# Gated mix of an S5 scan and hedgehog linear attention: the last two output tiles scaled in halves by two engines

## The chip, the cores and the metric

The kernel runs on one core of a Trainium2 chip. TensorE (PE) multiplies into PSUM, VectorE (DVE) and ScalarE (ACT) move and transform tiles between PSUM and SBUF, GpSimd (POOL) does small set-up work, and SyncE (SP) issues transfers; ACT can issue transfers from its own queue too. The metric is device time in microseconds, the median of several executions. Before the change it is 155.21 us (three executions, 154.76 to 155.4).

## What is computed

The input `x` has 2048 rows of 512 features. Two branches read it, and a gate mixes them row by row. Cut to what matters:

```python
g = sigmoid((x * gate_w).sum(-1, keepdims=True))
# branch a: a diagonal complex recurrence over the 2048 rows
h[t] = Lam_bar * h[t-1] + B_bar @ x[t]
a = 2.0 * real(hseq @ Cmat.T) + x * Dskip
# branch b: linear attention, 32 heads of 16, softmax feature maps of +p and -p
num = phi_q @ (phi_k.T @ v);  den = phi_q @ phi_k.sum(rows) + 1e-6
b = (num / den) @ wo
out = g * a + (1 - g) * b
```

All inputs and the output are bfloat16. The kernel takes `g` out of the sum: it accumulates `a` and `b * (1 - g) / g` in one PSUM tile and multiplies the whole by `g` at the end.

## The kernel before the change

The 2048 rows are cut into 16 tiles of 128 rows, numbered n = 0 to 15 in the order in which the output is made. Each stage is a Python generator that records a few instructions and yields; the string `ORDER` (line 24) is a list of tokens written out by hand, and line 804 walks it: each token runs its generator one step on. So the place of a token in the list sets where its instructions stand in each engine's queue. Behind a token, `@4` names the PSUM bank, `:D` gives a copy or scaling to VectorE instead of ScalarE, and `:A` sends a store from ScalarE's queue instead of SP's.

Early tokens load and transpose weights and `x`, build the recurrence, and run the key side of the attention. The last third makes the output, tile by tile, with three stages:

- `y` (`st_y`, line 711) opens the PSUM tile `py` (128x512, float32, one bank) and adds branch a to it: products at line 717 and the skip term at 722.
- `o` (`st_o`, line 725) makes the attention output of the tile: products into `pn` (736), logarithm `ld` of the denominators and copy `nu` of the numerators out of the same bank (739, 740), their quotient `on` (744), and its transpose `oT`. For n up to 11 a transfer does the transposing (758); for tiles 12 to 15 TensorE does it into `po` (753), and one copy, `oT` from `po` (755, through `evac`, lines 119 and 121), brings it to SBUF.
- `t` (`st_t`, line 761) has three steps: the products of `oT` with `Wo`, added to `py` (765); scaling of `py` by the gate column of `G` into the SBUF tile `ot` (769 on ScalarE, 771 on VectorE); and one store of `ot`, 128 KB, to the output in HBM (773).

The products of tile n can start only when its `oT` copy is done. The list ends with the products of tile 13, then the transposes of tile 14, the three steps of tile 15, the copy of tile 14 on VectorE, the products of tile 14, scaling and store of tile 13, and scaling and store of tile 14. In this ending all three scalings are on ScalarE; the stores of tiles 15 and 13 are issued by SP, that of tile 14 by ScalarE. Behind everything stands the closing of the program (line 843 in the profile): SP waits for the semaphore of every transfer lane, then all engines meet at a barrier.

Each transfer issued by ACT or SP takes the next of eight semaphore lanes in turn, so the lane of a store follows from its place among all transfers.

Of the kernel before, what the change touches and what calls it, by code (L numbers as in the profile page):

```python
# [10 lines left out]
ALU = mybir.AluOpType  # L11
# [3 lines left out]
BF16 = mybir.dt.bfloat16  # L15
# [5 lines left out]
P = 128  # L21
# [27 lines left out]
o10 S3 y14@3 S3 y14 t7 t7:D t8 y14 t8 y15@0 o11@4 S3 o11 o11@1 t9 o12@4 o11:D o11 S3 o10 o10 o12 o12@1 o12 o12 t9:D  # L49
o11 y15 o13@4 o13:D o13@6 t6:A o13 o13 o11 o12 y10@1 o14@4 y15 o14:D o12@6 t9 o12:D t7:A t1 y10 y10 o13 o15@4 o15  # L50
o15@6 t4:A t5 o15 o15 t8 o15 t12 t12 t12:A t10 o14@4 o14 o14 t10:D o13@6 t11 o15@2 o15 t10 o13:D t11 t11:A y13 t13 o14
o14@1 t15 t15 t15 o14:D t14 t13 t13 t14 t14:A
"""
H_VECTOR = tuple((r, j) for r in (1, 2, 4, 5, 6) for j in range(4))
OT_PE = (12, 13, 14, 15)
# [13 lines left out]
def kernel(  # L69
# [18 lines left out]
    nc = tc.nc  # L88
    _, S, D = A_x.shape
# [5 lines left out]
    NTI = S // P  # L95
# [10 lines left out]
    out_par = out2.rearrange("(a c r) d -> c r a d", r=NR, c=P)  # L106
    VT = nc.vector.tensor_tensor
    VS = nc.vector.tensor_scalar
# [70 lines left out]
    G = const.tile([P, NTI], F32, name="G")  # L179
# [280 lines left out]
    pools = {}  # L460
# [300 lines left out]
    def st_t(n):  # L761
        ti = order[n]
        py, oT = live["py", n], live["oT", n]
        for g in range(HG):
            MM(out=py[:], lhsT=oT[:, g, :], rhs=Wo[:, g, :], start=False, stop=(g == HG - 1))  # L765
        yield
        ot = pools["op"][1].tile([P, D], BF16, name="ot", bufs=14)
        if sel["eng"] == "act":
            nc.scalar.mul(out=ot[:], in_=py[:], mul=G[:, ti:ti + 1])  # L769
        else:  # L770
            VS(out=ot[:], in0=py[:], scalar1=G[:, ti:ti + 1], scalar2=None, op0=ALU.mult)
        yield
        sel["q"].dma_start(out=out_par[:, ti // 2, ti % 2, :], in_=ot[:])
        yield
# [17 lines left out]
    for n in range(NTI):  # L792
        st.update({f"k{n}": st_k(n), f"v{n}": st_v(n), f"q{n}": st_q(n), f"y{n}": st_y(n), f"o{n}": st_o(n), f"t{n}": st_t(n)})
# [54 lines left out]
```

## Time and profile before

| what | value |
|---|---|
| median of the executions | 155.21 us |
| the profiled execution's own time | 155.28 us |
| its span, first to last instruction | 153.2 us |
| granted TensorE clock, mean | 0.995 |
| TensorE matmul busy | 146.2 us, 95% |
| VectorE busy | 132.4 us, 86% |
| ScalarE busy | 129.2 us, 84% |
| HBM read and written | 2.64 MB and 2.10 MB |

The span is what the trace covers; the profiled execution's own time is 2.1 us more, which lies outside the trace. A row of the timeline is: start in us from the span's beginning, duration in us, engine, line, operation, output tile <- inputs, and in brackets the idle time of the engine before it with what ended that idle time. A `q` behind an engine's name (ACTq, SPq) marks its instruction queue: issuing a transfer, or waiting. A group row has the number of instructions, then total busy us and the mean ns of one, then the idle time before them.

### The profile page before, as it was taken

Reading aid. Unit: us, or ns where it says so; the run is one execution under the profiler, and the core shown is the slowest. Engines: PE = TensorE matmul, PEld = TensorE weight load, DVE = VectorE, ACT = ScalarE, POOL = GpSimd, SP = SyncE. Lnnn points to the kernel's source line nnn. Section 1 sums busy time; section 2 is a strip of 40 time slices with the busy share of each in tenths; the row PEclk is TensorE's granted clock in tenths of the full one; section 3 lists DMA queues with packets and bytes.
Section 4 is the critical chain, followed back from the end, with each engine's and each line's share of the span. In section 5 each row is a group of like instructions: output and inputs, shape, how many; then the busy total and the mean of one; then the engine's idle time right before and its main releaser. Section 6 shows DMA issues by size and latency. Waiting matters only on the chain.

```text
span 153.2 us, 3361 instructions
## 1 busy us (share of the span) xinstructions
PE 146.2 (95%) x1236; PEld 95.0 (62%) x1254; DVE 132.4 (86%) x303; ACT 129.2 (84%) x279; POOL 15.8 (10%) x43
## 2 busy tenths in 40 slices
PE   7899999999999999999999999999999999999990
PEld 7644434788878985869867656555554455555540
DVE  3799999999999999999999999999999958717520
ACT  3489998999998999999998999699498998627562
POOL 8239980000000000000000000000000000000000
PEclk9999999999999999999999999999999999999997
DMA  4875995534445699930000007711278859969842
GB/s 116 164 218 97 223 178 112 103 75 103 103 107 78 129 230 178 166 115 4 0 0 4 0 0 169 74 37 34 42 98 147 176 122 189 162 129 206 247 143 103
DMA packets 50848, 17.55 MB, mean 115 GB/s; under 512 B 44176, under 2 KB 50832, under 8 KB 50832
## 3 DMA queue, kind: packets, MB, share of 16 engines
q1 hardware_dynamic: 48976, 15.75, 53.8%
q10 hardware_dynamic: 1696, 1.57, 3.2%
q8 instruction: 10, 0.16, 0.5%
q0 software_dynamic: 160, 0.01, 0.2%
q14 instruction: 6, 0.05, 0.1%
HBM read 2.64 MB, written 2.10 MB: 31 GB/s over the span
## 4 chain that ended last, share of the span: by engine, by line
PE 78%; SPq 10%; DMA 7%; issue 1%; ACT 1%
PE pgq L601 18%; PE py L717 16%; PE pq L475 9%; PE py L765 8%; SPq L229 8%; PE pv L475 4%; PE ph L668 4%; PE pk L475 4%; DMA xT<-in_A_x_dram 4%; PE kvacc L578 3%; DMA phT<-EEq 3%; PE pn L736 3%; PE pgq L606 2%; PE py L722 2%; PE pgq L608 2%; SPq L284 1%
## 5 line engine op out<-in xcount | busy, mean ns | idle before, releaser
L601 PE MATMUL pgq<-xT,BT 128*128 128x256 bf16 x256 | 31.5, 272 | 0.0
L475 PEld LDWEIGHTS <-xT 128*128 128x128 bf16 x192 | 18.2, 98 | 18.3 <-DMA xT<-in_A_x_dram 0.7
L601 PEld LDWEIGHTS <-BT 128*128 128x128 bf16 x256 | 24.6, 98 | 4.1
L138 ACT ACTIVATE EEk<-EEk 128x1024 bf16<-128x1024 bf16 x20 | 20.4, 1080 | 0.0
L119 ACT CAST uv<-pgq 128x512 bf16<-128x512 f32 x28 | 15.9, 605 | 0.5 <-PE pgq L601 0.4
L475 PE MATMUL pv<-Wv,xT 128*128 128x512 bf16 x59 | 15.5, 379 | 0.3
L475 PE MATMUL pq<-Wq,xT 128*128 128x512 bf16 x60 | 15.4, 379 | 0.2
L765 PE MATMUL py<-Wo,oT 128*128 128x512 bf16 x62 | 15.3, 379 | 0.1
L475 PE MATMUL pk<-Wk,xT 128*128 128x512 bf16 x62 | 14.7, 379 | 0.3 <-DMA xT<-in_A_x_dram 0.2
L138 ACT ACTIVATE EEq<-EEq 128x1024 bf16<-128x1024 bf16 x12 | 11.7, 1042 | 0.3 <-DVE EEq L527 0.3
L769 ACT ACTIVATE ot<-py,G 128x512 bf16<-128x512 f32 x12 | 7.9, 686 | 4.5 <-PE py L765 4.3
L138 ACT ACTIVATE ld<-pn 128x16 f32<-128x16 f32 x32 | 6.1, 191 | 5.7 <-PE pn L736 4.6
L590 ACT ACTIVATE phT<-X,dgB 128x512 bf16<-128x512 bf16 x16 | 10.7, 725 | 0.0
L119 ACT CAST nu<-pn 128x256 bf16<-128x256 f32 x27 | 9.9, 380 | 0.0
L119 ACT CAST vx<-pv 128x512 bf16<-128x512 f32 x16 | 9.1, 604 | 0.4 <-PE pv L475 0.4
L548 DVE TENSOR_TENSOR EEk<-EEk,rck 128x4096 bf16<-128x4096 bf16 (+1 forms) x5 | 9.3, 1858 | 0.0
L744 DVE TENSOR_TENSOR on<-nu,rd 128x512 bf16<-128x512 bf16 x16 | 6.7, 421 | 2.8 <-ACT rd L138 1.6
L765 PEld LDWEIGHTS <-oT 128*128 128x128 bf16 x64 | 5.7, 97 | 5.3 <-DMA oT<-on 0.5
L119 ACT CAST Xq<-pq 128x512 bf16<-128x512 f32 x16 | 8.9, 608 | 0.0
L119 ACT CAST Xq<-pk 128x512 bf16<-128x512 f32 x15 | 8.6, 598 | 0.4 <-PE pk L475 0.4
L736 PEld LDWEIGHTS <-phT 128*128 128x128 bf16 x128 | 6.2, 97 | 3.8 <-DMA phT<-EEq 1.4
L511 DVE TENSOR_TENSOR smk<-smk 128x512 bf16<-128x512 bf16 (+4 forms) x18 | 8.1, 448 | 0.1
(178 smaller groups left out, 321.2 us busy)
## 6 DMA issues: line engine op xcount, KB each, us to landing
X<-HM SPq DMA_DIRECT2D x8, 256.0 KB, 4.5
out_dram<-ot ACTq DMA_DIRECT2D x8, 128.0 KB, 2.5
out_dram<-ot SPq DMA_DIRECT2D x8, 128.0 KB, 2.2
C2r<-in_B_wqkv_dram ACTq DMA_DIRECT2D x2, 256.0 KB, 3.8
Wv<-in_B_wqkv_dram SPq DMA_DIRECT2D x1, 512.0 KB, 4.0
Bn<-in_A_B_re_dram SPq DMA_DIRECT2D x1, 512.0 KB, 5.7
Bn<-in_A_B_im_dram SPq DMA_DIRECT2D x1, 512.0 KB, 6.8
Wo<-in_B_wo_dram SPq DMA_DIRECT2D x1, 512.0 KB, 4.3
```

Of the source, the lines that this page charges most:

```text
L119: nc.scalar.copy(out=out_ap, in_=in_ap)
L138: ins = nc.scalar.activation(**kw)
L229: nc.sync.dma_start_transpose(out=xT[:, :, ti * P:(ti + 1) * P], in_=x_res[ti // 2, ti % 2])
L475: MM(out=pt[:], lhsT=xT[:, kt, ti * P:(ti + 1) * P], rhs=W[:, kt, :], start=(kt == 0), stop=(kt == KT - 1))
L511: VT(out=dst, in0=cur[:, :, :, 0:n, :], in1=cur[:, :, :, n:2 * n, :], op=op)
L548: VT(out=E5, in0=E5, in1=rc.to_broadcast([P, L, 2 * NB, Dh, 4]), op=ALU.mult)
L590: nc.scalar.mul(out=t_, in_=x_, mul=c_)
L601: MM(out=pg[:, h, :], lhsT=BT[:, kt, 2 * j + h, :], rhs=xT[:, kt, r * NC:(r + 1) * NC], start=(h == 0 and kt == 0), stop=(r % 2 == 0 and k ...
L717: MM(out=py[:], lhsT=hs(r, t, slice(a * P, (a + 1) * P)), rhs=C2B[t], start=(t == 0), stop=False)
L736: MM(out=pn[:, 4 * m:4 * m + 4, :].rearrange("p h e -> p (h e)"), lhsT=ph[:, 4 * hf + m, :], rhs=KVm[:, 4 * hf + m, :], start=(m == 0), st ...
L765: MM(out=py[:], lhsT=oT[:, g, :], rhs=Wo[:, g, :], start=False, stop=(g == HG - 1))
L769: nc.scalar.mul(out=ot[:], in_=py[:], mul=G[:, ti:ti + 1])
```

## The change

The copy of tile 14's `oT` on VectorE (`o14:D`) moves in the list from behind the three steps of tile 15 to in front of them. For tiles 14 and 15 the scaling is cut into two halves of 256 columns: ScalarE scales columns 0 to 255 into a tile `oh0`, VectorE scales columns 256 to 511 into a tile `oh1`, each tile with two buffers; and each half has a store of its own (64 KB), the first from ScalarE's queue, the second from SP's. Tile 13 keeps its one scaling on ScalarE and its one store on SP.

```diff
-o14@1 t15 t15 t15 o14:D t14 t13 t13 t14 t14:A
+o14@1 o14:D t15 t15 t15 t14 t13 t13 t14 t14
 """
...
             MM(out=py[:], lhsT=oT[:, g, :], rhs=Wo[:, g, :], start=False, stop=(g == HG - 1))
         yield
+        if n >= NTI - 2:
+            ha = [pools["op"][1].tile([P, D // 2], BF16, name=f"oh{c}", bufs=2) for c in range(2)]
+            nc.scalar.mul(out=ha[0][:], in_=py[:, 0:D // 2], mul=G[:, ti:ti + 1])
+            VS(out=ha[1][:], in0=py[:, D // 2:D], scalar1=G[:, ti:ti + 1], scalar2=None, op0=ALU.mult)
+            yield
+            for c, q in enumerate((nc.scalar, nc.sync)):
+                q.dma_start(out=out_par[:, ti // 2, ti % 2, c * (D // 2):(c + 1) * (D // 2)], in_=ha[c][:])
+            yield
+            return
         ot = pools["op"][1].tile([P, D], BF16, name="ot", bufs=14)
```

The order of the built programs differs only in this ending. TensorE's list is the same, instruction for instruction. ScalarE's ends with: half of 15, its store, scaling of 13, half of 14, its store. VectorE's ends with: copy of 14, half of 15, half of 14. SP's ends with: half store of 15, store of 13, half store of 14, then the closing waits.

## Prediction

> **What bounds the kernel now.** I read the page first, for what carries the whole.
>
> ```profile
> span 153.2 us, 3361 instructions
> PE 146.2 (95%) x1236; PEld 95.0 (62%) x1254; DVE 132.4 (86%) x303; ACT 129.2 (84%) x279; POOL 15.8 (10%) x43
> PE 78%; SPq 10%; DMA 7%; issue 1%; ACT 1%
> ```
>
> TensorE carries 78% of the chain that ended last, and the change leaves its list alone. So only the ending can move. The chain of waits, from 148 us on:
>
> ```profile
> 147.88 0.45 PE py L765 x2
> 148.32 0.02 issue
> 148.34 0.89 ACT ot L769 x2
> 149.23 0.27 issue
> 149.50 0.69 ACT ot L769
> ```
>
> The products of tile 15 release the first scaling, and from there the chain stays on ScalarE. The timeline of the same stretch shows who waits (windows cut short, so that equal rows are not merged):
>
> ```profile
> 147.06 0.39 PE L753 MATMUL po<-ident,on 128*128 128x128 bf16 x4
> 147.48 0.42 DVE L121 COPY oT<-po 128x512 bf16<-128x512 bf16 x1 [1.06 <-PE po L753]
> 148.14 1.03 PE L765 MATMUL py<-Wo,oT 128*128 128x512 bf16 x4
> 148.34 0.69 ACT L769 ACTIVATE ot<-py,G 128x512 bf16<-128x512 f32 x1 [1.00 <-PE py L765]
> 148.93 1.25 ACT L769 ACTIVATE ot<-py,G 128x512 bf16<-128x512 f32 x2
> 149.06 0.33 SPq L773 DMA_DIRECT2D out_dram<-ot  x1
> 149.63 0.33 SPq L773 DMA_DIRECT2D out_dram<-ot  x1
> 149.50 0.69 ACT L769 ACTIVATE ot<-py,G 128x512 bf16<-128x512 f32 x1
> 150.22 0.34 ACTq L773 DMA_DIRECT2D out_dram<-ot  x1
> ```
>
> The scalings of 15, 13 and 14 start at 148.34, 148.93 and 149.50. TensorE's last product ends at 149.17, so tile 14 waits 0.33 us for ScalarE, which is still at tiles 15 and 13. ScalarE bounds this end: three scalings in a row, then one store, its landing, and the closing.
>
> **The change, part by part.** First the move of tile 14's copy. TensorE's transposes end at 147.45 and the copy starts at 147.48, with VectorE idle for 1.06 us before. Nothing else is in VectorE's queue in front of it, before or after: cost nothing. Its cover is its place ahead of the new half of tile 15: behind that half it would start after 149.2 instead of 147.48, and tile 14's products with it.
>
> Next, the halves. Durations of like operations, from the groups by shape:
>
> ```profile
> L769 ACT ACTIVATE ot<-py,G 128x512 bf16<-128x512 f32 x12 | 7.9, 686 | 4.5 <-PE py L765 4.3
> L119 ACT CAST vx<-pv 128x512 bf16<-128x512 f32 x16 | 9.1, 604 | 0.4 <-PE pv L475 0.4
> L119 ACT CAST nu<-pn 128x256 bf16<-128x256 f32 x27 | 9.9, 380 | 0.0
> L771 DVE TENSOR_SCALAR ot<-py,G 128x512 bf16<-128x512 f32 x4 | 3.0, 750 | 4.2 <-PE py L765 4.1
> L121 DVE CAST Wk<-pf 128x512 bf16<-128x512 f32 x2 | 1.4, 686 | 0.0
> L121 DVE CAST nu<-pn 128x256 bf16<-128x256 f32 x5 | 2.0, 423 | 2.6 <-ACT ld L138 2.6
> ```
>
> No row has a 256-column scaling. ScalarE's lies between its 256-column copy, 0.38, and that plus what scaling costs over copying at 512 columns (686 - 604 = 82 ns), 0.46. I take 0.45, near the end that is the same operation. VectorE's lies between 0.42 and 0.42 + (750 - 686) = 0.49; I take 0.46. Halving the columns saves far less than half the time.
>
> Then, do the halves run side by side? The last row above speaks against it. VectorE's copy `nu` reads other columns of `pn` than ScalarE's `ld`, needs nothing that `ld` makes, and yet 2.6 us of its idle time ended on `ld`. In the built list of the changed kernel (which has no times) VectorE's two halves likewise name ScalarE's semaphore, not TensorE's: reads of one PSUM tile by two engines are put behind one another. The Trainium skill, PSUM — Partial Sum Buffer, section "PSUM bank collisions raise a hardware error", says why: two engines on one bank and quadrant of partitions collide even when both only read, and at other addresses, so the compiler orders them; it would make the halves serial, as the `nu` row does, and separate destination tiles would not lift that. Without the rule, side by side, the sum would be the second rival's.
>
> So VectorE's half comes behind ScalarE's, after a hand-over:
>
> ```profile
> 145.55 0.41 ACT L138 ACTIVATE rd<-ld,nge 128x128 bf16<-128x128 f32 x1
> 146.00 0.43 DVE L744 TENSOR_TENSOR on<-nu,rd 128x512 bf16<-128x512 bf16 x1 [0.18 <-ACT rd L138]
> ```
>
> From ScalarE's end at 145.96 to VectorE's start at 146.00: 0.04 us. Scaling a tile then takes 0.45 + 0.04 + 0.46 = 0.95 us where it took 0.69.
>
> Next, the store that ScalarE now issues between tiles 15 and 13. It must wait for its half to finish, and whatever stands behind it in ScalarE's queue waits too: tile 13's scaling, then tile 14's half, then VectorE's half, the last store and the closing. What it costs is seen where the kernel already does it:
>
> ```profile
> 144.12 0.69 ACT L769 ACTIVATE ot<-py,G 128x512 bf16<-128x512 f32 x1
> 144.53 0.29 PE L736 MATMUL pn<-KVm,phT 128*128 128x68 bf16 x4
> 144.84 0.34 ACTq L773 DMA_DIRECT2D out_dram<-ot  x1
> 145.22 0.18 ACT L138 ACTIVATE ld<-pn 128x16 f32<-128x16 f32 x1 [0.41 <-PE po L753]
> ```
>
> The `ld` had its `pn` at 144.82 and the scaling ended at 144.81, yet `ld` began at 145.22, 0.04 after the issue ended. One store between two ScalarE instructions is a gap of 0.41 us.
>
> Now the sum on the path. Half of 15 from 148.34 to 148.79; gap 0.41; tile 13 starts at 149.20 (before: 148.93). Half of 14 follows 0.57 later, the distance of 13 and 14 before (149.50 - 148.93): 149.77 to 150.22. By then the products (149.17) are long done, so TensorE stays out of it. VectorE's half: 150.26 to 150.72. SP issues the last store about 0.03 later, the distance from 150.19 (end of tile 14's scaling) to 150.22: 150.75. SP's queue is free then: half store of 15 at about 149.3, tile 13's store at 149.20 + 0.68 + 0.03 = 149.9, each 0.33. So the last store is issued 0.53 us later than now. ScalarE's half store of 14 goes at 150.25 and is ahead of it.
>
> Next the landing (issues in windows around the last two SP stores, then around ScalarE's; the GB/s row is the stretch 149.9 to 151.7 in slices of 45 ns):
>
> ```profile
> out_dram<-ot SPq DMA_DIRECT2D x2, 128.0 KB, 1.9
> out_dram<-ot ACTq DMA_DIRECT2D x1, 128.0 KB, 2.0
> GB/s 205 319 364 364 319 364 341 273 228 69 23 0 68 182 319 341 364 364 341 364 296 183 69 23 0 23 205 296 341 341 364 364 364 296 205 91 23 0 0 0
> ```
>
> The last store's bytes move in the last 12 filled slices, 0.5 us of its 2.0; the rest is latency. No row has a 64 KB store of 512-byte rows. If bytes set its time it saves half of 0.5, landing in 1.75; if the 128 rows set it, nothing, 2.0. I take 1.86, between them. Landing is 152.61 instead of 150.22 + 2.0 = 152.22: 0.39 later.
>
> Last the closing. SP's waits in three windows, 150 to 150.25, then two rows from 152.2 to 152.4:
>
> ```profile
> L843 SPq EVENT_SEMAPHORE  x4: 17/28/28, 150.0 to 150.2; - x4
> L843 SPq EVENT_SEMAPHORE  x2: 28/28/28, 152.2 to 152.3; - x2
> L843 SPq DRAIN  x1: 13/13/13, 152.4 to 152.4; - x1
> ```
>
> SP goes through the lanes in a fixed order. Four that had long landed took three steps in 0.2 us, 0.067 each. Now the last store's lane is the seventh of eight: after it lands SP passes one more, then drains. The two new stores turn the lanes on: in the built list the last half store gets the first lane, named in the very first closing wait. After it lands six more passes follow where one did: five more, 5 x 0.067 = 0.33 us. By the rounding a step is 0.03 to 0.1, so 0.15 to 0.5.
>
> Sum: 0.39 + 0.33 = 0.72 us later. The profiled execution's own 155.28 becomes 156.0; it stands 0.07 above the median, so against that 155.93: I say 155.9. With all low ends (0.38 twice, 0.42, 1.75, 0.15) the sum is 0.26, with all high ends (0.46 twice, 0.49, 2.0, 0.5) 1.08: 155.5 to 156.3 by the median.
>
> **The rivals.** (1) The halved stores land later. Over all 16 stores of the kernel:
>
> ```profile
> DMA to landing us min/median/max: 1.9/2.3/3.9
> ```
>
> Tile 13's store and both of 14's now run within 0.85 us on two queues. If the last lands in the median 2.3, that adds 0.44: 156.4, slower. It decides when the bytes of one still move as the next begins. For it: the median itself. Against it: the last stores, already only 0.6 apart, land in 1.9 and 2.0.
>
> (2) The halves run side by side after all. VectorE's half of 14 would be done by 149.7, the last stores go out at 150.25, 0.50 earlier than forecast: 155.4, not measurably slower. For it: separate output tiles. Against: the `nu` row and the built list. It needs VectorE's half to start before ScalarE's ends.
>
> (3) The closing passes cost nothing, because the barrier waits for something else: 0.39 alone, 155.6. Against it: in the trace the drain comes 0.1 to 0.2 behind the last landing's wait.
>
> **How the numbers follow.** About 0.5%, 0.78 us, is what a measurement of this kernel can tell from no change, so the border lies at 155.99, just above my forecast. Chances: forecast 0.57, later landing 0.20, closing free 0.15, side by side 0.05, something that gains outright 0.03. Slower by over 0.5%: all of the first rival and some 0.25 of the forecast's 0.57, 0.45. Faster by over 0.5%: 0.03, since no term has an end below zero but for the second rival's. Within: 0.52. The range 155.4 to 156.4 takes in every bound and the second and third rivals.
>
> **What would show it.** Right: VectorE's half of 14 begins just after ScalarE's half ends; ScalarE stands 0.4 us between half 15 and tile 13; the last store goes out from SP near 150.75; about six closing waits follow its landing. The copy of tile 14 must stay at 147.5. Wrong: both halves starting together, a last issue before 150.3, or any row before 148 us that moves by more than some 0.1 us.

## The result, and the profile after

The changed kernel took 156.05 us (median of 11 executions, 155.63 to 157.47) against 155.21 for the kernel before: ratio 1.006, 95% interval 1.0034 to 1.0087. The forecast was 155.9. The profiled execution took 156.05 us over a span of 154.0.

A second set of executions of the same changed kernel, again beside the kernel before, gave 1.0029 (1.0004 to 1.0053). So the loss was measured twice, as 0.6% and as 0.3%; the two intervals overlap from 0.34% to 0.53%.

The timeline of the changed kernel's ending (start us, duration us, engine, line, operation, count, idle time before). Its lines 769 and 770 are the two halves, 773 their stores, 778 and 782 scaling and store of tile 13, and 852 the closing:

```profile
147.77 0.42 DVE L121 COPY oT<-po 128x512 bf16<-128x512 bf16 x1 [1.00 <-PE po L753]
148.63 0.47 ACT L769 ACTIVATE oh<-py,G 128x256 bf16<-128x256 f32 x1 [1.00 <-PE py L765]
149.13 0.34 ACTq L773 DMA_DIRECT2D out_dram<-oh  x1
149.14 0.48 DVE L770 TENSOR_SCALAR oh<-py,G 128x256 bf16<-128x256 f32 x1 [0.95 <-ACT oh L769]
149.52 0.69 ACT L778 ACTIVATE ot<-py,G 128x512 bf16<-128x512 f32 x1 [0.42 <-ACT oh L769]
149.65 0.33 SPq L773 DMA_DIRECT2D out_dram<-oh  x1
150.10 0.47 ACT L769 ACTIVATE oh<-py,G 128x256 bf16<-128x256 f32 x1
150.23 0.33 SPq L782 DMA_DIRECT2D out_dram<-ot  x1
150.60 0.34 ACTq L773 DMA_DIRECT2D out_dram<-oh  x1
150.60 0.48 DVE L770 TENSOR_SCALAR oh<-py,G 128x256 bf16<-128x256 f32 x1 [0.98 <-ACT oh L769]
151.12 0.33 SPq L773 DMA_DIRECT2D out_dram<-oh  x1
```

Each VectorE half (149.14, 150.60) begins when ScalarE's half of the same tile ends, although its products were done earlier. Between ScalarE's half of 15 and tile 13 stands the store's gap, 0.42 us. The last store leaves SP at 151.12.

All starts are later here (148.63 where it was 148.34); that arises ahead of the ending, in work that the change does not touch. Over these two kernels and all runs below whose code ahead of the ending is the same, that first start lies anywhere between 148.34 and 149.86 in the one profiled execution each. So I compare endings: from the start of tile 15's first scaling to the end of the span. An ending falls into three terms: to the issue of the last store, from there to its landing, and the closing from there to the end.

| kernel | to issue | landing | closing | ending us |
|---|---|---|---|---|
| before | 1.87 | 2.02 | 0.98 | 4.87 |
| changed | 2.49 | 1.65 | 1.28 | 5.41 |

(Each from the trace's times of that scaling, of the last store's issue and last semaphore write, and of the last instruction, to 0.01 us; rounding can leave 0.01.) The ending is 0.54 us longer, 0.35% of the time.

The last half store's landing (the row of the issues from 151.0 to 151.2), the rate of all transfers in slices of 45 ns from 150.6 to 152.4, and SP's closing waits from 151.4 on:

```profile
out_dram<-oh SPq DMA_DIRECT2D x1, 64.0 KB, 1.6
```

```profile
GB/s 341 251 194 91 23 0 0 0 0 0 137 250 319 387 319 364 341 341 228 228 262 319 307 251 205 103 12 0 0 11 148 228 330 284 228 160 57 12 0 0
```

```profile
L852 SPq EVENT_SEMAPHORE  x7: 28/28/1289, 151.5 to 153.1; - x7
L852 SPq DRAIN  x1: 13/13/13, 153.2 to 153.2; - x1
```

The last nine filled slices are the last half store's bytes: they move in 0.4 us, behind a short pause. The first closing wait holds SP for 1289 ns, from 151.5 until the last store has landed; six more passes (a pass is SP's wait for one lane; these lanes have landed by then) follow, the last starting at 153.1, before SP drains at 153.2. Before the change the last landing left one pass. And the groups by shape give what the trace of before had no row for:

```profile
L769 ACT ACTIVATE oh<-py,G 128x256 bf16<-128x256 f32 x2 | 0.9, 470 | 1.0 <-PE py L765 1.0
L770 DVE TENSOR_SCALAR oh<-py,G 128x256 bf16<-128x256 f32 x2 | 1.0, 484 | 1.9 <-ACT oh L769 1.9
```

Half the columns cost ScalarE 0.47 where the whole cost 0.69, and VectorE 0.48 where it cost 0.75.

### The profile page after: what moved, and what is told of

Its sections match the earlier page's. It is cut to its first block, busy times and chain, and to the rows that moved or that the text cites. A ratio compares the mean times of both kernels' runs of the same rounds, so it can differ in the third digit from the quotient of the medians.

```text
span 154.0 us, 3366 instructions
## 1 busy us (share of the span) xinstructions
PE 146.8 (95%) x1236; PEld 96.0 (62%) x1254; DVE 133.4 (87%) x305; ACT 129.0 (84%) x279; POOL 15.8 (10%) x43
## 4 chain that ended last, share of the span: by engine, by line
PE 73%; DVE 14%; DMA 6%; ACT 3%; issue 1%; ACTq 1%; DVEq 0%
PE pgq L601 18%; PE py L717 13%; PE pq L475 9%; PE py L765 7%; PE pv L475 4%; PE ph L668 4%; DMA oT<-on 3%; PE kvacc L578 3%; DMA phT<-EEq 3%; PE pgq L606 2%; DVE mnk L511 2%; PE spin L821 2%; PE pn L736 2%; DVE mxk L511 2%; PE py L722 2%; PE pgq L608 2%
## 5 line engine op out<-in xcount | busy, mean ns | idle before, releaser
L778 ACT ACTIVATE ot<-py,G 128x512 bf16<-128x512 f32 x10 | 6.8, 686 | 4.1 <-PE py L765 3.6
```

## The experiments

All endings in this section are split as in the table above. The runs with a ratio were compared with executions of the kernel before on the same chip; there its median was up to 0.75 us above the first set's, so ratios can be compared and times cannot.

**The changed kernel again**

> The changed kernel unaltered, on the same chip as the next three. If the loss is the ending alone (0.54 us of the span), the ratio to before is about 1.0035 and the ending is again 5.4. If something ahead of the ending is slower too, as the first profile hints (tile 15's first scaling at 148.63 in place of 148.34), the ratio stays at 1.006 or above.

Ratio 1.0029 (1.0004 to 1.0053), ending 2.49 + 1.65 + 1.27 = 5.41. The ending repeats to 0.01 us, and the ratio this time holds what the ending alone would give (0.35%); it is no second sign that something ahead of the ending is slower. In this trace the first scaling starts late again, at 148.59. But the kernel before has a single trace, and the spans of its executions in this set range from 153.0 to 155.5 us, so that start tells nothing.

**The copy back behind tile 15**

```diff
-o14@1 o14:D t15 t15 t15 t14 t13 t13 t14 t14
+o14@1 t15 t15 t15 o14:D t14 t13 t13 t14 t14
```

> The change without the move: the copy of tile 14 stands again behind tile 15's half on VectorE. The ending (from the start of tile 15's first scaling to the end of the span) is 4.87 us in the kernel before and 5.41 in the changed one. My theory, that the move is worth nothing by itself but shields the copy from the new half: VectorE's half of 15 ends about 0.99 after ScalarE's half begins, the copy then takes 0.42, tile 14's four products 0.86, its halves and the store as before: ending about 6.3, time about 156.9. Rival, the place in the list does not matter because the copy's inputs are ready early: 5.4, time 156.0.

Ratio 1.0117 (1.0068 to 1.0166), ending 3.47 + 1.65 + 1.27 = 6.40, near the 6.3 of the theory. The timeline shows why:

```profile
149.76 0.48 DVE L770 TENSOR_SCALAR oh<-py,G 128x256 bf16<-128x256 f32 x1 [2.50 <-ACT oh L769]
150.16 0.41 DVE L121 COPY oT<-po 128x512 bf16<-128x512 bf16 x1
150.64 1.04 PE L765 MATMUL py<-Wo,oT 128*128 128x512 bf16 x4 [1.42 <-DVE oT L121]
```

VectorE's queue holds the copy behind a half that waits 2.50 us, and TensorE then waits 1.42 us for the copy. The move brings nothing against the kernel before, but the halves need it: without it the ending is 0.99 longer.

**One load less, so the last store changes its lane**

```diff
-    for k0 in (0, 2):
-        nc.scalar.dma_start(out=wk_nat[:, k0:k0 + 2, :], in_=B_wqkv[k0 * P:(k0 + 2) * P, D:2 * D].rearrange("(k p) n -> p k n", p=P))
+    for k0 in (0,):
+        nc.scalar.dma_start(out=wk_nat[:, k0:k0 + 4, :], in_=B_wqkv[k0 * P:(k0 + 4) * P, D:2 * D].rearrange("(k p) n -> p k n", p=P))
```

> The change, with the two loads into C2r at the very start made one load of 512 KB, so that all later transfers take the lane before: the last store has the eighth lane and not the first. Ending and order of all engines are otherwise the same. Theory, that the passes over the lanes behind the last landing cost 0.30 us: from the last landing to the end of the span 0.92 us in place of 1.28, ending 5.05. Rival, that the closing waits for something else: 1.28 and 5.41. The whole time can also move by what the joined load does at the start (up to 0.5 either way), so the ending decides.

Ending 2.49 + 1.65 + 0.92 = 5.06. SP's waits at the end, from 151.5 on:

```profile
L852 SPq EVENT_SEMAPHORE  x7: 27/28/28, 151.6 to 152.9; - x7
L852 SPq DRAIN  x1: 13/13/13, 152.9 to 152.9; - x1
```

The seven passes are the same, but six of them now run while the last store is still on its way; the drain follows the landing at once. Only the closing moved, by 0.36. As a whole this kernel came out at 1.0065 (1.0034 to 1.0097), so the gain does not show in the whole time. Why is open: its one trace has no late start (TensorE's first `pk` products, line 475, begin at 7.65 us, in the changed kernel at 7.73).

**The same effect in the old ending**

```diff
-    for k0 in (0, 2):
+    for k0 in (0, 1, 2, 3):
```

(in the kernel before, with 128 rows of the weights to a load)

> The kernel before, with the two loads into C2r at the start cut into four, so that every later transfer takes the lane two on, and the last store has the first lane. Its ending is otherwise untouched. Theory of the passes: from the last landing to the end of the span 0.98 + 6 x 0.064 = 1.36, ending 5.25. Rival: 0.98 and 4.87.

One execution: ending 1.87 + 2.00 + 1.35 = 5.23. Issue and landing are those of the kernel before; the closing grew by 0.37 although nothing in the ending was touched:

```profile
L843 SPq EVENT_SEMAPHORE  x8: 17/28/28, 155.1 to 155.5; - x8
L843 SPq DRAIN  x1: 13/13/13, 155.6 to 155.6; - x1
```

All eight passes come after the landing. (The whole took 158.36 us; the start is later: TensorE waits for these loads, and its first `pk` products begin at 10.11 us instead of 7.67.) With the run before this settles the closing: 0.06 us a pass, and the lane of the last store decides how many are left.

**Both half stores of 15 from SP**

```diff
-            for c, q in enumerate((nc.scalar, nc.sync)):
+            for c, q in enumerate((nc.sync if n == NTI - 1 else nc.scalar, nc.sync)):
```

> The change, with both half stores of tile 15 from SP, so that ScalarE issues none between tiles 15 and 13. Theory, that this store holds ScalarE's queue: tile 13's scaling starts about 0.37 behind tile 15's half instead of 0.89, tile 14's half is bounded by its products (0.85 to 0.95 behind), the last store goes out about 0.5 earlier, ending 4.9, time 155.5. Rival, that the gap has another cause (the half must finish first): tile 13 still 0.89 behind, ending 5.4, time 156.0.

Ratio 1.0034 (1.001 to 1.0057), ending 1.96 + 2.15 + 1.27 = 5.38. The theory of the gap held and the forecast of the ending failed. ScalarE's two scalings now follow each other 0.37 apart, and the last store goes out 0.52 us earlier; but the stores of the end now look like this:

```profile
149.86 0.47 ACT L769 ACTIVATE oh<-py,G 128x256 bf16<-128x256 f32 x1 [1.00 <-PE py L765]
150.23 0.68 ACT L778 ACTIVATE ot<-py,G 128x512 bf16<-128x512 f32 x1
...
151.30 0.38 SPq L782 DMA_DIRECT2D out_dram<-ot  x1
151.30 0.37 ACTq L773 DMA_DIRECT2D out_dram<-oh  x1
...
151.82 0.36 SPq L773 DMA_DIRECT2D out_dram<-oh  x1
```

Tile 13's store and ScalarE's half of 14 leave at the same moment, and the last half half a microsecond later. The issues from 151.6 to 153.4, with their landings:

```profile
GB/s 0 0 80 193 296 296 262 194 103 34 0 0 11 148 273 319 364 284 364 341 307 319 319 353 330 262 330 285 285 262 285 228 114 46 0 0 0 0 0 0
out_dram<-ot SPq DMA_DIRECT2D x1, 128.0 KB, 2.5
out_dram<-oh ACTq DMA_DIRECT2D x1, 64.0 KB, 2.2
out_dram<-oh SPq DMA_DIRECT2D x1, 64.0 KB, 2.1
```

In slices of 45 ns the three stores move as one block without a pause, and each lands later: 2.5, 2.2 and 2.1 us. What ScalarE gained, the transfers took back: the ending is 0.03 shorter.

**The same without tile 13's store**

```diff
-        sel["q"].dma_start(out=out_par[:, ti // 2, ti % 2, :], in_=ot[:])
+        if n != NTI - 3:
+            sel["q"].dma_start(out=out_par[:, ti // 2, ti % 2, :], in_=ot[:])
```

> As the run with both half stores of 15 on SP, but tile 13's store is left out, so its 128 rows of the output are never written. That run issued its last store 0.52 us earlier than the changed kernel (1.96 behind tile 15's scaling) and yet gained only 0.04 in the ending, as the store landed in 2.15 in place of 1.65. Theory, that the landing grew because tile 13's store and ScalarE's half store were issued at the same moment: without tile 13's store the last half lands in 1.65 to 1.7; closing 0.92, as the last store has the eighth lane; ending 4.55. Rival, that half stores on two queues half a microsecond apart slow each other by themselves: landing 2.1, ending 5.0.

One execution: ending 1.96 + 1.64 + 0.92 = 4.53. The issue is the same, the landing is back at 1.64, and the closing is that of the eighth lane, as one store fewer is issued. The rival falls: two half stores half a microsecond apart do not slow each other; it was tile 13's store beside them.

**Halves for tile 14 alone**

```diff
-        if n >= NTI - 2:
+        if n == NTI - 2:
```

> Halves for tile 14 alone; tile 15 is scaled whole on ScalarE and stored from SP as before the change. The last store then has the eighth lane. Theory (terms add): tile 14's half starts 1.16 behind tile 15's scaling as in the kernel before, VectorE's half ends 0.98 later, store out at 2.17, landing 1.65 (64 KB), closing 0.92: ending 4.74, time 155.1, about 0.1 below the kernel before. Rival, that the halves of tile 14 are the loss themselves (landing no shorter than 2.0): ending 5.1, time 155.4.

Ratio 0.9999 (0.9975 to 1.0023), ending 2.17 + 1.71 + 0.92 = 4.81, 0.06 below the kernel before where 0.13 was expected; the landing was 0.06 longer than forecast. The halves of tile 14 pay for themselves and no more: the store goes out 0.30 later and lands 0.30 sooner. The 0.06 is one closing pass less, by the lane.

**Tile 13 on VectorE, no halves**

```diff
-o14@1 t15 t15 t15 o14:D t14 t13 t13 t14 t14:A
+o14@1 t15 t15 t15 o14:D t14 t13:D t13 t14 t14:A
```

> The kernel before, with tile 13's scaling on VectorE, behind tile 14's copy; no halves. Theory, that ScalarE's three scalings in a row bound the old ending: tile 14's whole scaling starts when its products end, 0.86 behind tile 15's, store out at 1.57, landing 2.0, closing 0.98, ending 4.56, time 0.3 below before (ratio 0.998). VectorE's scaling of 13 runs while ScalarE scales 15, as they read different PSUM tiles. Rival, that TensorE's last product or the landing sets the end: 4.87, ratio 1.000.

Ratio 0.9982 (0.9961 to 1.0003), ending 1.58 + 2.22 + 0.98 = 4.78. The issue came as forecast, 0.29 earlier; the landing grew by 0.20. Tile 13's result was ready early, but its store stood behind tile 15's in SP's queue, and the three stores left at 149.39, 149.81 and 150.26.

**Tile 13 on VectorE, tile 14 in halves (VectorE second, then ScalarE second)**

```diff
-o14@1 o14:D t15 t15 t15 t14 t13 t13 t14 t14
+o14@1 o14:D t15 t15 t15 t14 t13:D t13 t14 t14
...
-        if n >= NTI - 2:
+        if n == NTI - 2:
```

> Tile 13 whole on VectorE, tile 15 whole on ScalarE, tile 14 alone in halves as in the change. Tile 13's store then goes out early, and the two half stores of 14 have the queues to themselves. Theory, that the half stores land in 1.65 when nothing else moves: ScalarE's half starts 0.86 behind tile 15's scaling, VectorE's half ends at 1.82, store at 1.85, closing 0.92: ending 4.45. Rival, that two half stores half a microsecond apart land in 2.1 by themselves, as in the run with both stores of 15 on SP: 4.9.

Ratio 1.0001 (0.9965 to 1.0036), ending 1.88 + 1.92 + 0.92 = 4.72. For the second of the two, VectorE's line is replaced as well and the queues are exchanged:

```diff
-            VS(out=ha[1][:], in0=py[:, D // 2:D], scalar1=G[:, ti:ti + 1], scalar2=None, op0=ALU.mult)
+            nc.scalar.mul(out=ha[1][:], in_=py[:, D // 2:D], mul=G[:, ti:ti + 1])
...
-            for c, q in enumerate((nc.scalar, nc.sync)):
+            for c, q in enumerate((nc.sync, nc.scalar)):
```

> As the run before (tile 13 on VectorE), but both halves of tile 14 on ScalarE, the first stored by SP, the second by ScalarE. Theory, that following instructions of one engine overlap and need no hand-over: second half starts 0.37 behind the first, ends at 0.86 + 0.37 + 0.47 = 1.70, store at 1.73, landing 1.65 to 1.85 as the two stores are 0.37 apart, closing 0.92 to 0.98: ending 4.3 to 4.5, the best of all. Rival, that VectorE is the better second engine: above 4.5.

Ratio 0.9987 (0.996 to 1.0014), ending 1.73 + 2.06 + 0.91 = 4.71. In both the issue was as forecast to 0.03 us and the landing was not: 1.92 and 2.06. Two halves on one engine are done sooner than on two (1.73 against 1.88), because the second starts 0.37 behind the first without a hand-over; but of the three kernels with tile 13 on VectorE each has its last landing 3.80 behind tile 15's scaling, however early the last store is issued. Both forecasts of the landing failed, and something else than the last issue set it. The next two runs ask whether it is the stores in front.

**Tile 13's store in front**

```diff
-o14@1 t15 t15 t15 o14:D t14 t13 t13 t14 t14:A
+o14@1 o14:D t13:D t13 t15 t15 t15 t14 t14 t14:A
```

> The kernel before with tile 13's scaling on VectorE and its store ahead of tile 15's in SP's queue; no halves. With tile 13 on VectorE alone the store of 13 waited behind that of 15 in SP's queue, the three stores went out 0.43 apart and the last landed in 2.2. Theory, that the three stores of the end are now short of transfer time: issued at about 0.25, 0.71 and 1.58, the last has the engines to itself and lands in 2.0, closing 0.98: ending 4.56, ratio 0.998. Rival, that the last landing is fixed near 3.8 by something else: 4.78.

Ratio 0.9944 (0.991 to 0.9978), ending 1.58 + 1.88 + 0.98 = 4.45, with a landing 0.12 shorter than forecast. This kernel is faster than the kernel before by 0.2% to 0.9%; it was not run beside the changed one, which was slower than the kernel before both times. The same list with the two ScalarE halves of the run before:

```diff
-o14@1 o14:D t15 t15 t15 t14 t13:D t13 t14 t14
+o14@1 o14:D t13:D t13 t15 t15 t15 t14 t14 t14
```

> As the run before, with tile 14 scaled by ScalarE in two halves, the first stored by SP at 1.37, the second by ScalarE at 1.73. Theory: nothing else moves then, landing 1.65 to 1.85, closing 0.92: ending 4.3 to 4.5, ratio 0.996 to 0.998, the best of all. Rival as before: 4.7 or more.

Ratio 0.9973 (0.9937 to 1.0009), ending 1.73 + 1.67 + 0.91 = 4.31, the shortest. Timeline and landing of the first of the two:

```profile
148.24 0.74 DVE L771 TENSOR_SCALAR ot<-py,G 128x512 bf16<-128x512 f32 x1
148.76 0.69 ACT L769 ACTIVATE ot<-py,G 128x512 bf16<-128x512 f32 x1 [1.00 <-PE py L765]
149.01 0.81 SPq L773 DMA_DIRECT2D out_dram<-ot  x2
149.62 0.69 ACT L769 ACTIVATE ot<-py,G 128x512 bf16<-128x512 f32 x1 [0.18 <-PE py L765]
150.34 0.34 ACTq L773 DMA_DIRECT2D out_dram<-ot  x1
```

```profile
out_dram<-ot ACTq DMA_DIRECT2D x1, 128.0 KB, 1.9
```

The rate of the transfers around the last store, first with tile 13 on VectorE alone (150.9 to 152.7), then with its store in front (150.6 to 152.4), in slices of 45 ns:

```profile
GB/s 364 364 296 273 273 251 296 364 341 387 319 319 364 228 114 23 0 0 0 0 0 0 0 0 0 0 0 0 0 0 0 0 0 0 0 0 0 0 0 0
GB/s 341 341 205 91 23 0 0 0 0 0 0 0 0 182 273 387 341 364 319 341 341 251 91 23 0 0 0 0 0 0 0 0 0 0 0 0 0 0 0 0
```

VectorE is still scaling tile 13 when ScalarE starts on 15, SP has begun both its stores (149.01 and 149.47) before tile 14's scaling begins, and the last store has the transfers to itself. The issue is 1.58 in both kernels and the landing falls from 2.22 to 1.88, so the rival falls: the stores in front had set it. They do not hold up the last store's bytes, which end about 1.35 us behind its issue in both rows; but without the pause the landing comes about 0.85 behind the last byte, with it about 0.55. What takes this time no run shows. ScalarE waits 0.18 us for TensorE before tile 14: the three scalings no longer bound the end. The ending explains 0.42 us, 0.27%; the ratio's interval holds that at its edge (0.9978 against 0.9973) and its middle says more, for which the ending has no cause. Which of the two kernels is better is not settled: the second has the shorter ending by 0.13 us, and the intervals overlap.

## Why the prediction was right, and where a term was off

The direction and the mechanism came out, and the median came near the forecast (155.9 forecast, 156.05 measured); the ending grew by 0.54 us where 0.72 was forecast. By its own steps:

- **TensorE's list and the move cost nothing.** Tile 14's copy finds VectorE idle for 1.00 us (1.06 before), so nothing stands in front of it. The cover was real: taking the move back cost 0.99 us of ending.
- **Halves in series.** Shown by the trace: 1.9 us of VectorE's idle time ended on ScalarE's halves. The rule of the Trainium skill (PSUM — Partial Sum Buffer, "PSUM bank collisions raise a hardware error") agrees with it: both engines read one bank. No run tried what the hardware does without the wait. Tile 13's scaling on VectorE, from another bank, did run beside ScalarE's.
- **Scaling one tile: 0.95 us forecast, 0.98 measured** (150.10 to 151.08). The half times were 0.02 too low each.
- **ScalarE's store in the queue: 0.41 forecast, 0.42 measured**, and gone when the store went to SP (start distance 0.37 in place of 0.89).
- **Last issue: 0.53 later forecast, 0.61 measured** (from unrounded times). The missing 0.08 is three halves of 0.02 each, 0.015 between the starts of tile 13 and of tile 14's half (0.585 for 0.57), and 0.01 of the gap; the hand-over was 0.01 shorter than forecast (0.03).
- **Landing: 0.14 sooner forecast, 0.37 measured.** This is the term that was mis-sized. The forecast took 2.0 us as what a 128 KB store needs and let at most half of the 0.5 us go in which its bytes move. But the 2.02 of the kernel before held a wait behind other stores: the first of its last three stores landed in 1.89 and the next two in 2.00 and 2.02, and the last one landed in 1.88 once tile 13's store was in front. The half store landed in 1.65, and in 1.64 to 1.67 in five further runs that kept other stores away from it. So some 0.14 of the 0.37 is that wait, and 0.23 the smaller store, close to the 0.25 of the forecast's low end. The Trainium skill (DMA: Bandwidth & Descriptors, "Anatomy of one DMA — SWDGE (gpsimd) path") would give an estimate of 0.15 for 64 KB less, by a rate fitted for another issuing path; here the measurement decides.
- **Closing: 0.33 later forecast, 0.30 measured**, five more passes, and confirmed from both sides by the two runs that changed nothing in the ending but the lanes.

The errors of issue and landing have opposite signs, so the sum was 0.72 for 0.54 measured in the ending. The median came out 0.84 higher, 0.30 more than the ending, and no step of the prediction accounts for that; in the second set of executions it was 0.29%, about 0.45 us. That 155.9 lies so near to 156.05 is in part luck. The border at 155.99 was just passed in the first set and not reached in the second. (The low ends add up to 0.25, not 0.26; nothing hangs on it.)

One sign of being wrong did come: rows before 148 us moved by more than 0.1 us, tile 14's copy from 147.48 to 147.77, and with them the last issue to 151.12. As said with the repeated run, one trace each can't tell such a shift from the spread of the kernel before, so the sign was set too tight to test the mechanism.

Of the rivals: halves side by side and a free closing did not occur. The landing that grows by contention did not occur for the changed kernel's last store, but it took back the gain of the first improvement tried: when the 0.42 us gap that spaced the stores was taken away, the last store's landing went from 1.65 to 2.15.

## What to carry to other kernels

Two engines that read one PSUM tile were put behind one another here, so splitting a short last step over them gained no time in the scaling: 0.98 us for the two halves against 0.69 for the whole. Giving the engines different tiles let them run side by side. Before speeding up the instruction ahead of a last store, look at what else is in flight then: here an issue 0.52 us earlier was worth 0.03 while tile 13's store went out beside it, and with tile 13's store moved to the front the ending fell by 0.33 (4.78 to 4.45) at the same issue. And compare endings, not totals, when the change sits in the last few per cent of a kernel: totals of the changed kernel differed by 1.8 us within one set, its ending by less than 0.01 between two profiles.

## What was not expected of the hardware

The closing depends on how many transfers the kernel issues, even ones at its start: two more loads put the last store on the first semaphore lane, and from the last landing to the end it took 1.35 us instead of 0.98. And how long a store takes to land depends on what went out before it: the same 128 KB store, issued 1.58 us into the ending, landed in 2.22 us close behind another and in 1.88 with a pause before it, though its bytes were through equally soon. With a pause, a 64 KB store in 512-byte rows landed in 1.65, some 0.23 us sooner.
